# Weighted sums five blocks behind the scores, query tiles of 512 columns, six buffers of turned weights

## The chip, the cores and the metric

One core of a Trainium2 chip runs the program once. The metric is the device time of one execution in microseconds (us), given as the median of several runs. One execution was profiled; every time inside the program is read from that one.

The engines are PE (TensorE, matrix products and transposes), DVE (VectorE), ACT (ScalarE), POOL (GpSimd) and SP (SyncE, which here only issues DMA transfers). SBUF is the on-chip memory in which tiles lie, PSUM the accumulators of PE.

## What is computed

Attention with pooled keys, then a small network on the 128 highest-scoring rows of each batch:

```python
kv_pool = kv.reshape(B, H // r, r, W // r, r, C).mean(axis=(2, 4))   # B=4, H=384, W=32, r=4, C=128
k = v = kv_pool.reshape(B, -1, C) @ w_sr                              # 768 keys per batch
s = (q @ k.transpose(0, 2, 1)) / np.sqrt(C)                           # q: (4, 12288, 128)
a = np.exp(s - s.max(-1, keepdims=True))
a /= a.sum(-1, keepdims=True) + 1e-09
x = a @ v
...
for b in range(B):                                                    # capacity = 128
    top_idx = np.argpartition(-scores[b], capacity)[:capacity]        # scores = x . w_gate
    xe = x[b, top_idx]
    ye = np.maximum(xe @ w1, 0.0) @ w2                                # 128 -> 1024 -> 128
    out[b, top_idx] = xe + sigmoid(scores[b, top_idx])[:, None] * ye
```

## The kernel before

The 12288 queries of a batch are cut into 48 blocks of 256 columns (QT = 2 tiles of 128), 192 blocks over the four batches. One loop (lines 631 to 688) runs over the blocks. Iteration i does these things:

- On even i, `load_q` (line 135) issues the DMA that loads the queries of blocks i+8 and i+9 (512 columns, 256 KB) into a quarter of a query tile. A query tile holds 2048 columns, and pool `qp` has two of them.
- `s_max(i)`: DVE takes the negated row maxima of the scores (the TENSOR_REDUCE `m<-s`, one per block, so a block's start can be read from it).
- `AV(i - LAG, 0)` and `AV(i - LAG, 1)`: PE forms the weighted sums of the block LAG back, 36 matmuls of 128x130 into the one PSUM tile `o_two`. They need that block's weights turned by 90 degrees, tile `at`, and the values `vx`. LAG is 4 (line 630). While i < LAG, `warm` puts 36 matmuls of ones there instead (line 648).
- On even i, `split_q(i + 2)` splits the queries of two blocks into a high part (ACT, `qh`) and a low part (POOL, `ql`).
- `S(i + 1)`: PE forms the next block's scores, 12 matmuls of 512 or 256 columns (three passes of high and low parts), and between them, in batches 0 to 2, `turn_pe` turns two 128x128 pieces of the weights (`ae`) on PE.
- `exp(i, ...)` (ACT) forms the weights; `to_high` (ACT, `hl`) and `to_low` (POOL, and DVE for the part turned on PE) split them into a high and a low half of 16 bits. Line 402, `turn`, issues one DMA transpose per half, which turns `hl` into `at`. So each block has two DMA transposes, 384 in all.
- `sums`, `recip` and `finish` (DVE) divide `o_two` of block i - LAG by the row sums and put it into `x`; after every second block a DMA stores `x` (line 438) and POOL copies four columns of scores to `sc`.
- At fixed points (`at_point`) a step of a side task runs: the next batch's keys (`prep`: POOL sums `kv_sum`, then products), the first batch's values (`vals`), and `topk`, the choice of the 128 rows of a finished batch and the small network on them. `topk(b)` starts when the last block of batch b has been summed, that is in iteration 48(b+1) - 1 + LAG; its step in the next iteration forms sortable integers `key` from the scores with two DVE instructions on 128x96.

Every engine but SP executes in the order in which the code calls it. SP issues in order too, but the order of its issues is set by the scheduler when the program is built. Line 52 is the helper through which all compute instructions go, so nearly every row shows L52 and is told apart by its tile names.

The pools that hold a block's intermediate tiles are `hlp` (4 buffers of `hl`) and `at` (5 buffers). Before the loop `first_keys` loads the queries of the first 2048 columns as one transfer of 512 and one of 1536 columns. Behind the loop (lines 689 to 777) come the weighted sums of the last four blocks, into `o_all` (which is `o_two`) and into three spare pieces of the score buffers, then the choice of rows and the network for the last batch, partly by shorter steps of their own.

Of the kernel before, what the change touches and what calls it, by code (L numbers as in the profile page):

```python
# [6 lines left out]
F32 = mybir.dt.float32  # L7
# [12 lines left out]
P = 128  # L20
# [5 lines left out]
CHUNK = 2048  # L26
JPC = CHUNK // P
NCH = N // CHUNK
QT = 2
BLK = QT * P  # L30
NBLK = N // BLK
BPC = CHUNK // BLK
VC = C + 2
# [33 lines left out]
def attention_topk_mlp(ctx, tc, a, outs, capacity):  # L67
    nc = tc.nc
# [4 lines left out]
    kvp = ctx.enter_context(tc.tile_pool(name="kvp", bufs=3))  # L73
    kvs = ctx.enter_context(tc.tile_pool(name="kvs", bufs=2))
    keys = ctx.enter_context(tc.tile_pool(name="keys", bufs=2))
    qp = ctx.enter_context(tc.tile_pool(name="qp", bufs=2))
    qs = ctx.enter_context(tc.tile_pool(name="qs", bufs=3))
    wk = ctx.enter_context(tc.tile_pool(name="wk", bufs=3))
    wke = ctx.enter_context(tc.tile_pool(name="wke", bufs=2))
    hlp = ctx.enter_context(tc.tile_pool(name="hlp", bufs=4))  # L80
    at = ctx.enter_context(tc.tile_pool(name="at", bufs=5))
    ob = ctx.enter_context(tc.tile_pool(name="ob", bufs=3))
    sm = ctx.enter_context(tc.tile_pool(name="sm", bufs=4))
    tk = ctx.enter_context(tc.tile_pool(name="tk", bufs=2))
# [15 lines left out]
    s_buf = [ps_s.tile([P, KT, BLK], F32, name=f"s{i}") for i in range(2)]  # L100
# [3 lines left out]
    o_all = o_two[:, :, 0:VC]  # L104
# [15 lines left out]
    def load_kv(b, kc, parts=1, t=None):  # L120
        late = t is not None
        if not late:
            t = kvp.tile([P, 2, P // 2, TAPS], F32, name="kv_raw")
        n = 2 // abs(parts)
        for i in range(abs(parts)):
            if parts > 0 or late == (i > 0):
                nc.sync.dma_start(out=t[:, i * n:(i + 1) * n], in_=a["kv"][:, b, kc, i * n:(i + 1) * n])
        return t

    qraw = {}  # L130

    def load_q(b, ch, lo=0, hi=CHUNK):
        if (b, ch) not in qraw:
            qraw[b, ch] = qp.tile([P, CHUNK], F32, name="q_raw")
        nc.sync.dma_start(out=qraw[b, ch][:, lo:hi], in_=a["q"][:, b, ch, lo:hi])

    kvset = {}

    def new_keys(b):
        kvset[b] = {  # L140
            "kh": keys.tile([P, M], F32R, name="kh"),
            "kl": keys.tile([P, M], BF16, name="kl"),
            "kb": keys.tile([P, M], BF16, name="kb"),
            "raw": keys.tile([P, KT, 2, P], F32, name="kv_proj"),
            "vw": keys.tile([P, KT], F32, name="vw"),
            "mx": keys.tile([P, 4], F32, name="mx"),
            "vx": keys.tile([P, 2, KT, VC], F16, name="vx"),
            "sg": keys.tile([P, 4], F32, name="sg"),
        }

    def project(pooled, ps):
        pe.matmul(ps[:, 0], w_k, pooled, start=True, stop=True)
        pe.matmul(ps[:, 1], pooled, w_sr, start=True, stop=True)

    def split_k(b, lo, hi, part):
        kv = kvset[b]
        kh, kl, kb = (kv[k][:, lo * P:hi * P].rearrange("p (t k) -> p t k", k=P) for k in ("kh", "kl", "kb"))
        raw = kv["raw"][:, lo:hi, 0]
        if part == 0:
            act.copy(kh, raw)  # L160
            act.copy(kb, raw)
        else:
            kv["split"] = hi
            pool.tensor_tensor(out=kl, in0=raw, in1=kh.bitcast(F32), op=ALU.subtract)

    def v_gate(b, kc, v=None):
        u = kvs.tile([P, C], F32, name="vw_prod")
        dve.scalar_tensor_tensor(out=u, in0=kvset[b]["raw"][:, kc, 1] if v is None else v, scalar=1.0, in1=wg, op0=ALU.mult, op1=ALU.mult, accum_out=kvset[b]["vw"][:, kc:kc + 1])

    def v_max(b, pair):  # L170
        kv = kvset[b]
        dve.tensor_reduce(out=kv["mx"][:, pair:pair + 1], in_=kv["raw"][:, 2 * pair:2 * pair + 2, 1], axis=AX.XY, op=ALU.max, apply_absolute_value=True)
# [41 lines left out]

    def first_keys():
        new_keys(0)
        load_q(0, 0, 0, 2 * BLK)
        raws = [load_kv(0, kc) for kc in range(3)]
        nc.sync.dma_start(out=cst, in_=a["cst"])
        raws += [load_kv(0, kc, 2) for kc in range(3, KT)]  # L220
        load_q(0, 0, 2 * BLK, CHUNK)
        split_q(0, 0)
        kv = kvset[0]
        for kc in range(KT):
            pooled = kvs.tile([P, P], F32, name="pooled")
            for h in range(2):
                dve.tensor_reduce(out=pooled[:, h * P // 2:(h + 1) * P // 2], in_=raws[kc][:, h], axis=AX.X, op=ALU.add)
            if kc == 4:
                dve.tensor_copy(tri16, tri)
            if kc > 1:  # L230
                v_gate(0, kc - 2)
            if kc == 3:
                v_max(0, 0)
            ps = banks[kc % 2][:, 0:2 * P].rearrange("p (a b) -> p a b", a=2)
            if kc < KT - 1:
                project(pooled, ps)
                act.copy(kv["raw"][:, kc], ps)
                split_k(0, kc, kc + 1, 0)
                split_k(0, kc, kc + 1, 1)
            else:  # L240
                warm(4, banks[0][:, 0:P])
                project(pooled, ps)
                kh, kl, kb = (kv[k][:, kc * P:(kc + 1) * P] for k in ("kh", "kl", "kb"))
                dve.tensor_copy(kh, ps[:, 0])
                act.copy(kb, ps[:, 0])
                dve.tensor_tensor(out=kl, in0=ps[:, 0], in1=kh.bitcast(F32), op=ALU.subtract)
                act.copy(kv["raw"][:, kc, 1], ps[:, 1])
                warm(8, banks[1][:, 0:P])
        S(0)
        S(1)  # L250
# [67 lines left out]
    xt_ = {}  # L318

    def split_q(b, blk):  # L320
        ch, h = divmod(blk, BPC)
        raw = qraw[b, ch][:, h * BLK:(h + 2) * BLK]
        qh = qs.tile([P, 2 * BLK], F32R, name="qh")
        ql = qs.tile([P, 2 * BLK], BF16, name="ql")
        act.copy(qh, raw)
        pool.tensor_tensor(out=ql, in0=raw, in1=qh.bitcast(F32), op=ALU.subtract)
        for i in range(2):
            h, l = (x[:, i * BLK:(i + 1) * BLK] for x in (qh, ql))
            qsplit[b, blk + i] = h, h.bitcast(BF16).rearrange("p (q s) -> p q s", s=2)[:, :, 1], l

    blocks = [(b, blk) for b in range(B) for blk in range(NBLK)]
# [274 lines left out]
    blocks = [(b, blk) for b in range(B) for blk in range(NBLK)]  # L606
# [7 lines left out]
    def start(tasks, gen):  # L614
        tasks.append([gen, next(gen)])
# [11 lines left out]

    start(vals, first_values())
    nb = len(blocks)
    LAG = 4  # L630
    for i in range(nb):
        old = i >= LAG
        b, blk = blocks[i]
        if blk % 2 == 0 and i + BPC < nb:
            nb_, nblk = blocks[i + BPC]
            load_q(nb_, nblk // BPC, nblk % BPC * BLK, (nblk % BPC + 2) * BLK)
        if blk == 0 and b + 1 < B:
            start(prep, next_keys(b + 1))
        if i:
            borrow(s_flat[(i - 1) % 2])  # L640
        s_max(i)
        if old:
            AV(i - LAG, 0)
            at_point("pe")
            AV(i - LAG, 1)
        else:
            at_point("pe")
            warm(18 if i == 0 else 36, banks[0][:, 0:P])
        if i % 2 == 0 and i + 2 < nb:
            split_q(*blocks[i + 2])  # L650
        InOrder.seen.clear()
        at_point("ev")
        bank1 = list(InOrder.seen)
        InOrder.seen.clear()
        at_point("up")
        at_point("t")
        at_point("cmp")
        at_point("g")
        more = 0 < i < nb - 1
        bank0 = list(InOrder.seen)  # L660
        if more:
            S(i + 1, (3,), bank0 + bank1)
            S(i + 1, (2,), bank0)
        exp(i, 1)
        exp(i, 2)
        if by_pe(i):
            exp(i, 0)
            turn_pe(i)
        if more:
            S(i + 1, (1,), bank0)  # L670
            S(i + 1, (0,))
        to_high(i, 1)
        if old:
            sums(i - LAG)
            recip(i - LAG)
            finish(i - LAG)
        to_low(i, 1, dve)
        if not by_pe(i):
            exp(i, 0)
        to_high(i, 0)  # L680
        turn(i, 0)
        to_low(i, 0, pool)
        turn(i, 1)
        at_point("d")
        if i in (1, 2):
            advance(vals, "d")
        if old and blocks[i - LAG][1] == NBLK - 1:
            start(select, topk(blocks[i - LAG][0]))
    ended.append(True)
    room["select"], room["count"] = banks[1], banks[0][:, 0:1]  # L690
    n = nb - 1
    b = blocks[n][0]
    spare = [s_buf[(n + 1) % 2][:, 2 * k:2 * k + 2].rearrange("p k q -> p (k q)")[:, 0:QT * VC].rearrange("p (j c) -> p j c", j=QT) for k in range(3)]
    dest = {n - 3: o_all, n - 2: spare[0], n - 1: spare[1], n: spare[2]}

    def out(m):
        for j in range(QT):
# [20 lines left out]
    for j in range(3):  # L718
        pool.memset(jt[:, j:j + 1], float(j + 1))

    for m in (n - 3, n - 2):
        out(m)
        norm(m)
        put(m)
# [3 lines left out]
    for m in (n - 1, n):  # L728
        norm(m)
        lo = blocks[m][1] * QT  # L730
# [78 lines left out]
```

## Time and profile before

| | us |
|---|---|
| three runs | 977.23, 981.31, 986.22 |
| their median | 981.31 |
| the profiled execution, whole | 983.61 |
| its span, first to last record | 981.8 |
| PE busy | 908.2 (93 % of the span) |
| POOL busy | 749.9 (76 %) |
| ACT busy | 729.5 (74 %) |
| DVE busy | 699.7 (71 %) |

The busy share counts the time in which an engine has an instruction under way, waits left out. A row that ends in "[1.25 <-DMA at<-hl]" tells that the engine sat idle for 1.25 us before the instruction, and what ended that. "at<-hl" reads as "tile at, made from tile hl". The granted clock is TensorE's clock as a share of its full speed.

### The profile page before, as it was taken

Reading aid. Unit: us, or ns where it says so; the run is one execution under the profiler, and the core shown is the slowest. Engines: PE = TensorE matmul, PEld = TensorE weight load, DVE = VectorE, ACT = ScalarE, POOL = GpSimd, SP = SyncE. Lnnn points to the kernel's source line nnn. Section 1 sums busy time; section 2 is a strip of 40 time slices with the busy share of each in tenths; the row PEclk is TensorE's granted clock in tenths of the full one; section 3 lists DMA queues with packets and bytes.
Section 4 is the critical chain, followed back from the end, with each engine's and each line's share of the span. In section 5 each row is a group of like instructions: output and inputs, shape, how many; then the busy total and the mean of one; then the engine's idle time right before and its main releaser. Section 6 shows DMA issues by size and latency. Waiting matters only on the chain.

```text
span 981.8 us, 26115 instructions
## 1 busy us (share of the span) xinstructions
PE 908.2 (93%) x10067; PEld 729.7 (74%) x10067; DVE 699.7 (71%) x1732; ACT 729.5 (74%) x1177; POOL 749.9 (76%) x573
## 2 busy tenths in 40 slices
PE   3889999999989999998999998999999999999944
PEld 2668777787768787776787876877787887777743
DVE  6456666666668777776767776777768887878674
ACT  2567887877967877877877866878789988988700
POOL 1478889888778988987888887898778877777600
PEclk9999999999989999999999999999999999999966
DMA  9999999999999999999989999999999999999910
GB/s 357 227 190 220 241 220 224 244 242 236 225 203 186 249 226 219 233 230 225 235 169 210 236 218 226 207 199 203 199 184 245 224 242 244 231 235 234 225 40 6
DMA packets 600508, 211.31 MB, mean 215 GB/s; under 512 B 532288, under 2 KB 582592, under 8 KB 599616
## 3 DMA queue, kind: packets, MB, share of 16 engines
q1 hardware_dynamic: 600128, 209.12, 104.4%
q8 instruction: 79, 1.29, 0.6%
q0 software_dynamic: 256, 0.52, 0.2%
q14 instruction: 45, 0.37, 0.1%
HBM read 52.04 MB, written 25.43 MB: 79 GB/s over the span
## 4 chain that ended last, share of the span: by engine, by line
PE 56%; DVE 13%; ACT 9%; DMA 8%; issue 4%; POOL 3%; SPq 1%; POOLq 0%; ACTq 0%; DVEq 0%
PE s L52 31%; PE o_two L52 25%; DVE m L52 8%; DMA at<-hl 7%; ACT am L52 5%; POOL hl L52 1%; DVE junk L52 1%; ACT ae L52 1%; ACT hl L52 1%; ACT at L52 1%; POOL ql L52 1%; DVE at L52 1%; DMA xe<-out,idx 1%; POOL kv_sum L52 1%; ACT s L52 1%
## 5 line engine op out<-in xcount | busy, mean ns | idle before, releaser
L52 POOL TENSOR_TENSOR hl<-am,hl 128x1280 bf16<-128x1280 f32 x192 | 503.7, 2623 | 153.6 <-ACT hl L52 75.4
L52 PEld LDWEIGHTS <-at 128*128 128x128 f16 (+1 forms) x6912 | 415.5, 97 | 71.4 <-DMA at<-hl 22.5
L52 PE MATMUL o_two<-vx,at 128*128 128x130 f16 x6804 | 435.0, 220 | 17.5 <-DMA at<-hl 12.9
L52 ACT ACTIVATE am<-s,m 128x512 f32<-128x512 f32 (+1 forms) x384 | 305.4, 795 | 140.6 <-DVE m L52 80.9
L52 DVE TENSOR_REDUCE m<-s 128x2 f32<-128x1536 f32 x192 | 337.1, 1756 | 24.8 <-PE s L52 20.8
L52 PE MATMUL s<-kl,qh 128*128 128x512 bf16 (+1 forms) x768 | 253.3, 333 | 0.0
L52 PE MATMUL s<-kh,qh 128*128 128x512 f32 (+1 forms) x768 | 251.8, 409 | 0.0
L52 PE MATMUL s<-kb,ql 128*128 128x512 bf16 (+1 forms) x768 | 248.7, 327 | 0.5 <-POOL ql L52 0.4
L52 ACT CAST hl<-am 128x1280 f16<-128x1280 f32 x192 | 245.1, 1276 | 1.5
L52 DVE TENSOR_TENSOR at<-s,at 128x256 bf16<-128x256 f32 x144 | 61.1, 425 | 132.5 <-ACT at L52 124.4
L52 PEld LDWEIGHTS s<-kh,qh 128*128 128x128 f32 x768 | 131.6, 192 | 30.5 <-issue 0.6
L52 POOL TENSOR_TENSOR ql<-q_raw,qh 128x512 bf16<-128x512 f32 x96 | 122.5, 1276 | 6.8 <-ACT qh L52 6.8
L52 PEld LDWEIGHTS <-qh 128*128 128x128 bf16 x768 | 75.3, 98 | 63.2 <-issue 62.4
L52 DVE TENSOR_TENSOR x<-o_two,rz 128x260 f32<-128x260 f32 x189 | 81.0, 429 | 10.0
L52 PEld LDWEIGHTS <-ql 128*128 128x128 bf16 x768 | 76.2, 99 | 3.7 <-POOL ql L52 1.1
L52 DVE TENSOR_SCALAR rz<-o_two,sg 128x2 f32<-128x2 f32 x189 | 41.1, 218 | 40.2 <-PE o_two L52 39.3
L52 PE MATMUL s<-cst,ae 128*128 128x128 f32 x288 | 61.6, 296 | 8.4 <-ACT ae L52 7.7
L52 ACT ACTIVATE ae<-s,m 128x256 f32<-128x256 f32 x144 | 67.3, 467 | 0.0
L52 ACT CAST at<-s 128x256 f16<-128x256 f32 x144 | 54.5, 379 | 16.4 <-PE s L52 15.0
L52 ACT CAST qh<-q_raw 128x512 fp32r<-128x512 f32 x96 | 60.6, 631 | 1.1 <-DMA q_raw<-in_q 1.1
L52 PEld LDWEIGHTS s<-cst,ae 128*128 128x128 f32 x288 | 30.4, 141 | 32.0 <-ACT ae L52 31.4
L52 POOL TENSOR_TENSOR kv_sum<-kv_raw 128x256 f32<-128x256 f32 x72 | 52.4, 727 | 0.0
(164 smaller groups left out, 557.4 us busy)
## 6 DMA issues: line engine op xcount, KB each, us to landing
out<-x SPq DMA_DIRECT2D x96, 256.0 KB, 3.4
q_raw<-in_q SPq DMA_DIRECT2D x93, 256.0 KB, 3.8
kv_raw<-in_kv SPq DMA_DIRECT2D x36, 512.0 KB, 5.4
kv_raw<-in_kv SPq DMA_DIRECT2D x6, 1024.0 KB, 7.4
at<-hl SPq DMA_TRANSPOSE x384, 4.0
w<-in_w SPq DMA_DIRECT2D x2, 512.0 KB
q_raw<-in_q SPq DMA_DIRECT2D x1, 768.0 KB, 7.6
cst<-in_cst SPq DMA_DIRECT2D x1, 320.0 KB
```

Of the source, the lines that this page charges most:

```text
L52: r = f(*args, **kwargs)
```

## The change

LAG goes from 4 to 5, so that the weighted sums of a block run one iteration later, and `at` gets a sixth buffer for it. The queries come into tiles of 512 columns, one for each pair of blocks, in four buffers. The amount of data and the iteration in which a load is called are as before; a load takes a buffer of its own instead of a quarter of one, and the 1536 columns of the beginning become three transfers of 512. Behind the loop a fifth block is left to sum, into a fourth spare piece of a score buffer.

```diff
-    qp = ctx.enter_context(tc.tile_pool(name="qp", bufs=2))
+    qp = ctx.enter_context(tc.tile_pool(name="qp", bufs=4))
...
-    at = ctx.enter_context(tc.tile_pool(name="at", bufs=5))
+    at = ctx.enter_context(tc.tile_pool(name="at", bufs=6))
...
-    def load_q(b, ch, lo=0, hi=CHUNK):
-        if (b, ch) not in qraw:
-            qraw[b, ch] = qp.tile([P, CHUNK], F32, name="q_raw")
-        nc.sync.dma_start(out=qraw[b, ch][:, lo:hi], in_=a["q"][:, b, ch, lo:hi])
+    def load_q(b, blk):
+        ch, h = divmod(blk, BPC)
+        qraw[b, blk] = qp.tile([P, 2 * BLK], F32, name="q_raw")
+        nc.sync.dma_start(out=qraw[b, blk], in_=a["q"][:, b, ch, h * BLK:(h + 2) * BLK])
...
-        load_q(0, 0, 0, 2 * BLK)
+        load_q(0, 0)
...
-        load_q(0, 0, 2 * BLK, CHUNK)
+        for blk in range(2, BPC, 2):
+            load_q(0, blk)
...
-        raw = qraw[b, ch][:, h * BLK:(h + 2) * BLK]
+        raw = qraw.pop((b, blk))
...
-    LAG = 4
+    LAG = 5
...
-            nb_, nblk = blocks[i + BPC]
-            load_q(nb_, nblk // BPC, nblk % BPC * BLK, (nblk % BPC + 2) * BLK)
+            load_q(*blocks[i + BPC])
...
+    spare.append(s_buf[n % 2][:, 4:6].rearrange("p k q -> p (k q)")[:, 0:QT * VC].rearrange("p (j c) -> p j c", j=QT))
-    dest = {n - 3: o_all, n - 2: spare[0], n - 1: spare[1], n: spare[2]}
+    dest = {n - 4: o_all, n - 3: spare[0], n - 2: spare[1], n - 1: spare[2], n: spare[3]}
...
-    for m in (n - 3, n - 2):
+    for m in range(n - LAG + 1, n - 1):
```

What this does to the order of the instructions shows at three places.

On PE in iteration 4, in front of the scores of block 5 (`s_111`; `o_two` is the tile of weighted sums, `ones` a tile of ones):

```order
 L52 LDWEIGHTS ql
 L52 MATMUL s_110<-kb,ql 128x512
-L52 LDWEIGHTS at
-L52 MATMUL o_two<-vx,at 128x130
...
+L52 LDWEIGHTS ones_108
+L52 MATMUL o_two<-ones_108 128x128
...
 L52 LDWEIGHTS qh
 L52 MATMUL s_111<-kl,qh 128x512
```

The 36 pairs of the first weighted sums have left iteration 4 for iteration 5, and 36 pairs on ones stand there.

On SP, four blocks of the first batch; before:

```order
L402 DMA_TRANSPOSE at_1725<-hl_1724 128x10x128 x2
L135 DMA q_raw_2056<-in_q 128x512 x4
L402 DMA_TRANSPOSE at_1802<-hl_1801 128x10x128 x2
L438 DMA out_0<-x_1819 128x4x128
L402 DMA_TRANSPOSE at_1877<-hl_1876 128x10x128 x2
L402 DMA_TRANSPOSE at_1959<-hl_1958 128x10x128 x2
L438 DMA out_0<-x_1976 128x4x128
```

and after:

```order
L402 DMA_TRANSPOSE at_1732<-hl_1731 128x10x128 x2
L135 DMA q_raw_1910<-in_q 128x512
L438 DMA out_0<-x_1749 128x4x128
L402 DMA_TRANSPOSE at_1809<-hl_1808 128x10x128 x2
L402 DMA_TRANSPOSE at_1885<-hl_1884 128x10x128 x2
L135 DMA q_raw_2064<-in_q 128x512
L438 DMA out_0<-x_1902 128x4x128
L402 DMA_TRANSPOSE at_1967<-hl_1966 128x10x128 x2
```

The four loads of a query tile, which stood together between the transposes of two blocks, now stand one by one, one for every two blocks.

On POOL, about the start of the first batch's `topk` (`th` and `tl` are set at its start; on DVE its `key` pair stands behind the low half of block 52 before, of block 53 now; `hl_4252` and `hl_4267` are block 52's); before:

```order
L52 TENSOR_TENSOR hl_4170<-am_4169,hl_4170 128x1280
L52 TENSOR_TENSOR kv_sum_3895<-kv_raw_3890 128x256
L52 MEMSET th_4198 128x1
L52 MEMSET tl_4200 128x1
L52 TENSOR_TENSOR ql_4242<-q_raw_3264,qh_4241 128x512
L52 TENSOR_TENSOR hl_4252<-am_4251,hl_4252 128x1280
L52 TENSOR_TENSOR kv_sum_3895<-kv_sum_3895 128x128x4
```

and after:

```order
L52 TENSOR_TENSOR ql_4257<-q_raw_3741,qh_4256 128x512
L52 COPY sc_759<-x_4207 128x4
L52 TENSOR_TENSOR hl_4267<-am_4266,hl_4267 128x1280
L52 TENSOR_TENSOR kv_sum_3912<-kv_sum_3912 128x128x4
L52 MEMSET th_4294 128x1
L52 MEMSET tl_4296 128x1
L52 TENSOR_TENSOR hl_4343<-am_4342,hl_4343 128x1280
```

The start of `topk` has moved from the iteration that holds a `ql` to the next, which holds none.

## Rows read from the trace of the kernel before

**Rows 1.** The page: the span, each engine's busy time with its share and instructions.

```profile
span 981.8 us, 26115 instructions
PE 908.2 (93%) x10067; PEld 729.7 (74%) x10067; DVE 699.7 (71%) x1732; ACT 729.5 (74%) x1177; POOL 749.9 (76%) x573
```

**Rows 2.** The chain that ended last, one undisturbed block of batch 0 and the scores of a block of batch 3: start, duration, engine, tile, instructions.

```profile
183.32 2.06 PE o_two L52 x36
185.38 2.39 PE s L52 x14
...
754.84 2.03 PE s L52 x12
```

**Rows 3.** The waits of PE from 50 to 922 us: who waits <- for whom: us in all, times, longest.

```profile
PE o_two L52 <- DMA at<-hl: 12.9, 22, 2.2
...
PE s L52 <- ACT ae L52: 6.7, 11, 3.5
...
PE o_two L52 <- POOL vx L52: 2.5, 2, 2.2
```

**Rows 4.** The same view for three stretches: 400 to 470, 520 to 610 and 780 to 890 us, one row each.

```profile
PE o_two L52 <- DMA at<-hl: 3.0, 6, 1.4
...
PE o_two L52 <- DMA at<-hl: 4.7, 4, 2.2
...
PE o_two L52 <- DMA at<-hl: 4.5, 10, 1.2
```

**Rows 5.** The timeline of iterations 3 and 4: start, duration, engine, line, operation, tiles; in brackets the idle time before the row and what ended it.

```profile
45.66 2.17 PE L52 MATMUL o_two<-ones 128*128 128x128 bf16 x36
...
50.52 0.45 PE L52 MATMUL o_two<-vx,at 128*128 128x130 f16 x5
...
50.72 1.76 DVE L52 TENSOR_REDUCE m<-s 128x2 f32<-128x1536 f32 x1
...
54.02 0.65 POOL L52 TENSOR_TENSOR vx<-kv_proj,vx 128x256 f16<-128x256 f32 x1
...
54.72 2.52 PE L52 MATMUL o_two<-vx,at 128*128 128x130 f16 x27 [2.23 <-POOL vx L52]
...
60.35 1.76 DVE L52 TENSOR_REDUCE m<-s 128x2 f32<-128x1536 f32 x1 [0.20 <-PE s L52]
```

**Rows 6.** The view of tile `at`: its DMA transposes on SP, their duration there in ns (shortest, median, longest), first and last start.

```profile
L402 SPq DMA_TRANSPOSE at<-hl x384: 1252/1423/5044, 34.3 to 931.0; - x192
```

**Rows 7.** The timeline of SP's queue and of PE in the stretch up to 606 us, where the longest waits of batch 2 lie.

```profile
593.17 2.22 SPq L135 DMA_DIRECT2D q_raw<-in_q  x4
...
595.50 4.60 SPq L402 DMA_TRANSPOSE at<-hl  x2
...
604.41 0.52 PE L52 MATMUL o_two<-vx,at 128*128 128x130 f16 x6 [1.02 <-DMA at<-hl]
```

**Rows 8.** The waits of SP's query loads from 50 to 922 us, columns as in rows 3.

```profile
SPq L135 <- POOL ql L52: 4.8, 6, 1.2
```

**Rows 9.** Three windows, each with its length, then the busy time (instructions) of PE, PEld, DVE, ACT and POOL, the granted clock, the DMA share and GB/s.

```profile
55.40:58.80 3.40, 3.40 (x25) 2.66 (x22) 0.82 (x3) 0.00 (x0) 1.18 (x1) 0.50 0.73 182
...
284.00:291.00 7.00, 5.58 (x39) 4.59 (x40) 4.05 (x12) 4.93 (x9) 3.44 (x4) 0.51 1.18 214
...
604.90:608.40 3.50, 3.50 (x26) 2.77 (x23) 1.51 (x7) 0.12 (x1) 1.66 (x2) 0.51 1.18 263
```

**Rows 10.** The timeline about iteration 52, the start of the first batch's `topk`: DVE, POOL and one row of PE.

```profile
269.99 1.76 DVE L52 TENSOR_REDUCE m<-s 128x2 f32<-128x1536 f32 x1
...
274.45 1.76 DVE L52 TENSOR_REDUCE m<-s 128x2 f32<-128x1536 f32 x1
...
275.24 2.63 POOL L52 TENSOR_TENSOR hl<-am,hl 128x1280 bf16<-128x1280 f32 x1 [0.44 <-POOL sc L52]
...
278.58 1.28 POOL L52 TENSOR_TENSOR ql<-q_raw,qh 128x512 bf16<-128x512 f32 x1
...
278.78 1.15 DVE L52 TENSOR_SCALAR key<-sc 128x96 int32<-128x96 int32 x1
...
279.82 2.62 POOL L52 TENSOR_TENSOR hl<-am,hl 128x1280 bf16<-128x1280 f32 x1
...
279.96 2.59 DVE L52 TENSOR_TENSOR key<-key,sc 128x96 int32<-128x96 int32 x1
...
282.39 1.29 POOL L52 TENSOR_TENSOR kv_sum<-kv_sum 128x512 f32<-128x512 f32 x1
...
282.48 1.75 DVE L52 TENSOR_REDUCE m<-s 128x2 f32<-128x1536 f32 x1
...
285.42 0.69 PE L52 MATMUL s<-cst,ae 128*128 128x128 f32 x2 [3.48 <-ACT ae L52]
...
293.84 1.76 DVE L52 TENSOR_REDUCE m<-s 128x2 f32<-128x1536 f32 x1 [0.19 <-PE s L52]
```

**Rows 11.** The timeline of DVE in batch 1, the start of its `topk`: the second `key` instruction.

```profile
511.22 0.26 DVE L52 TENSOR_TENSOR key<-key,sc 128x96 int32<-128x96 int32 x1
```

**Rows 12.** The timeline of PE behind the loop: the weighted sums of the last blocks.

```profile
925.10 2.22 PE L52 MATMUL o_two<-vx,at 128*128 128x130 f16 x36 [0.97 <-DVE x L52]
...
933.36 0.85 PE L52 MATMUL s<-vx,at 128*128 128x130 f16 x12 [0.77 <-DMA at<-hl]
934.71 1.55 PE L52 MATMUL s<-vx,at 128*128 128x130 f16 x24 [0.49 <-DMA at<-hl]
```

More of the change, by code (lines that the diff above doesn't have):

```diff
@@ L320, in split_q @@
     def split_q(b, blk):
-        ch, h = divmod(blk, BPC)
-        raw = qraw[b, ch][:, h * BLK:(h + 2) * BLK]
+        raw = qraw.pop((b, blk))
         qh = qs.tile([P, 2 * BLK], F32R, name="qh")
```

## The prediction, made before the kernel was run

> **What bounds the kernel now.** The page first [rows 1]: PE is busy for 908.2 of 981.8 us, the others for about 700 to 750. So PE is the engine to follow, and 73.6 us in which it is idle are all that better order can win, besides stretches in which its clock is low. The profiled execution took 983.6 us, 2.3 above the median shown; the sum below is made against 983.6.
>
> Then the chain of waits, for one undisturbed block [rows 2]: 2.06 us of weighted sums and 2.39 us of scores follow each other, 4.45 us, and nothing else stands in the chain. In batch 3, without PE's transposes, the scores take 2.03, so a block takes some 4.1. The change removes no matrix product, so this floor stays. What can move lies in the blocks that take longer.
>
> The waits of PE inside the loop [rows 3] name three causes: turned weights that come late (12.9 us, 22 times), the transposes of `ae` that wait for ACT (6.7 us, of which one wait is 3.5), and the values' low half `vx` (2.5 us, two waits). I looked up where each lies. The late weights come in clusters: three stretches hold 3.0, 4.7 and 4.5 of the 12.9 us [rows 4]. The wait for `vx` is at the first weighted sums [rows 5]. The 3.5 us wait is at the start of the first batch's `topk` [rows 10].
>
> **Part 1: the first weighted sums move from iteration 4 to 5.** In iteration 4 PE began them at 50.52 and stopped; the last 27 matmuls waited 2.23 us for a `vx` that POOL had begun at 54.02 and took 0.65 us over, so it was there at 54.67 [rows 5]. The next row maximum came at 60.35, 9.63 us after the one of 50.72 [rows 5]; of that, 5.18 us are over the 4.45 of an ordinary block. Right after the wait the granted clock was 0.50, the 1.2 GHz level, for 3.4 us [rows 9], and this is inside the 9.63. Afterwards 36 matmuls of ones stand there, 2.17 us in the row of iteration 3 [rows 5], and wait for nothing. The first weighted sums begin about 50.5 + 4.45 = 54.95, later than 54.67. Gain: 5.2 us. Should they be called somewhat early, the wait is some tenths; if the clock falls all the same, 3.4 us at half speed give away 1.7. Bounds 3.3 to 5.2; I take 5.2, since the `vx` chain does not depend on the weighted sums.
>
> **Part 2: a block more of time for turned weights, and queries in single loads.** On SP four query loads take 2.22 us, and the two transposes behind them 4.60 [rows 7], where two median ones take 2.85 [rows 6]. So a group of four loads makes the transposes behind it about 2.22 + 1.75 = 4.0 us late, and the next group comes eight blocks on. Undisturbed, a block's two transposes and its share of two small loads and stores take some 3.4 us of SP (2.85, and half of 0.55 twice), so SP makes up about 1.0 us a block, and less beside the large key loads. That is how the waits come to stand in clusters: the queue does not run empty in between. Now one load stands between the transposes at a time; the same lateness comes in pieces of about 1 us, every second block. And a block's weights are needed 4.45 us later (4.1 in batch 3). A wait moves PE back, so within one cluster the waits add up to what the queue had fallen behind: 3.0, 4.7 and 4.5 us [rows 4]. Against 4.45, 4.45 and 4.1 this leaves 0.3 and 0.4 us, even without the evener loads. I take 11.9 of the 12.9 us as gained. Bounds: 3, if the queue falls behind as long as it is loaded (rival C), and 12.9.
>
> A query load must now wait until POOL has split the pair whose buffer it takes, and the transposes of the following blocks are queued behind it on SP. Such waits exist: 4.8 us in six [rows 8], the longest 1.2. With loads every second block they are more, but a transpose that is 1.2 us late has 4.45 us more to be so. I take nothing for it; without that cover it costs up to 1.2 each time. What would be late next is `hl`: it keeps four buffers, so a block's is wanted again four iterations on, now before its turned weights are.
>
> In batch 2 the clock fell after such a wait: 0.51 for 3.5 us from 604.9 [rows 9], behind the wait of 1.02 us at 604.41 [rows 7]. Without the wait it should stay up: 3.5 x 0.49 = 1.7 us gained (bounds 0 and 1.7).
>
> **Part 3: the start of the first `topk` moves by one iteration.** The row maxima of 274.45 and 293.84 lie 19.39 us apart, three blocks of 4.45 would be 13.35: 6.04 us were lost [rows 10]. The reason stands in the same rows. The two `key` instructions of DVE take 1.15 and 2.59 us; in batch 1 the second takes 0.26 [rows 11]. Here they lie under POOL's `ql` (278.58, 1.28 us) and `hl` (279.82, 2.62 us) and end with them. The row maximum slips to 282.48, ACT's `ae` comes late, PE waits 3.48 us, and the clock is 0.51 from 284 to 291 [rows 9, 10]. The Trainium skill, "SBUF — State Buffer", section "Who interferes with whom", says that VectorE and GpSimd share one port pair as an exclusive lock; by that rule, whichever starts first holds the other up, and the rows agree, 2.59 us instead of 0.26.
>
> Now `key` is formed in iteration 53, odd, without `ql`. What does POOL do there? In the odd iteration 51 `hl` began 275.24 - 269.99 = 5.25 us after the row maximum [rows 10], and `key` begins about 278.78 - 274.45 = 4.33 after it. Iteration 52's `hl` then ends at 5.25 + 2.62 - 4.45 = 3.4 us, and the `kv_sum` behind it, 1.29 us, at about 4.7. Between 4.7 and 5.25 lie 0.5 us, and the pair needs 0.20 + 0.26: it just fits. So this is a close race: gain 5.5 if it is won (some tenths of slip remain), about nothing if `hl` starts ahead of the second instruction. I take 5.5, and the other end is rival B. The starts of batches 1 and 2 move in the same way.
>
> **Part 4: behind the loop.** A block more is summed there, 2.06 us, and one more sum into a new piece waits for DVE's `x`, as the 0.97 us wait shows [rows 12], though the pieces are mostly free. Against this, the sums of the last two blocks now wait 0.77 + 0.49 us for their transposes [rows 12] and have more work ahead of them. And the loop loses one weighted sum (2.06) at its beginning, which the ones fill (2.17), so no time there. Net I take +1.5, bounds 0 and 3. The steps of batch 2's and 3's `topk` that run with it move by one step, some tenths either way.
>
> **Sum.** 983.6 - 5.2 - 11.9 - 1.7 - 5.5 + 1.5 = 960.8 us. The runs shown scatter from 977 to 986, as stalls that hang on a close race would; a version without the stalls ends where they are gone, so I don't move it by the 2.3 us to the median.
>
> **The rivals.**
> - *A, the forecast:* 952 to 964.5, chance 0.55. The lower end is where other small excesses go too (the waits of 0.2 to 1 us for `ae`, 3.2 us in all beyond the long one, and the tail at nothing).
> - *B, the race of part 3 is lost, there or at another start or end of `topk`:* one collision is 6.0 us, so 960.8 + 5.7 = 966.5. For it: both POOL spans press on a gap of 0.5 us. Against it: batch 1's start passed with 0.26 [rows 11]. Chance 0.25.
> - *C, SP or the DMA rings set the rate, and a block more only puts the waits off:* three quarters of the late weights stay, so part 2 gives 3 and no clock: 983.6 - 5.2 - 3 - 5.5 + 1.5 = 971.4. For it: a transpose took up to 5.0 us where 1.4 is the median [rows 6], and the bytes are the same. Against it: 3.4 us of 4.45 undisturbed, and the waits lie in three stretches, not everywhere [rows 4]. The Trainium skill, "DMA: Bandwidth & Descriptors", section "Latency and other measured facts", gives an effective 261 GB/s for a DMA transpose; an estimate by it for a block's 655,360 bytes is 2.5 us, which would speak against C as well. Chance 0.13.
> - *D, slower:* the new parity puts `topk`'s other DVE pairs under POOL's `hl`. There are six such places, the starts and the ends of the search in three batches, and each would cost 6.0 us with its clock. With k of them the time is about 960.8 + 6 k: four give 984.8, no faster than before, and six 996.8. For it: they all move together by one iteration, and a pair that lies under `hl` is ten times as long [rows 10, 11]. Against it: POOL's load differs from batch to batch, as the same pair in batch 1 shows. Chance 0.07.
>
> **How the numbers follow.** The likeliest is A, 960.8, and I put the time at 960.5. The range 952 to 973 holds A, B and most of C, some 0.85 with their edges taken off; what is left out is D and the ends. One per cent, 9.8 us, is about what a measurement of this kernel can tell from no change: faster lies below 971.5. A and B lie below it, and half of C; with their tails faster has 0.82. The rest of C and D up to four places make 0.13 for within 1%; more places than that, 0.05 for slower.
>
> **What would show it.** Right: PE goes through iterations 3 to 6 without a wait, and the row maxima of blocks 4 and 5 lie under 5 us apart (part 1). PE's waits for `at` are under 2 us in all, and SP's query loads stand singly (part 2). The second `key` instruction of batch 0 takes 0.26 us, and the clock is at 1.0 from 60 to 920 us (part 3). The end of the loop to the end of the span is 1 to 2 us longer than now (part 4). Wrong: waits for `at` of more than 5 us (C), `key` or the pair at the end of the search at 1 us or more (B, D), or ACT or POOL waiting for a free `hl`, which the sum holds at nothing.

## The result

| | median us | range | runs |
|---|---|---|---|
| before | 982.25 | 977.23 to 986.22 | 15 |
| changed | 988.39 | 982.13 to 990.74 | 15 |

The ratio is 1.006, with a 95 % interval of 1.0043 to 1.0078: 6 us slower where some 21 us faster was forecast, and 15 us above the top of the range. The profiled execution of the changed kernel took 988.03 us.

The page of the changed kernel, as [rows 1]:

```profile
span 986.3 us, 26072 instructions
PE 899.8 (91%) x9922; PEld 727.5 (74%) x10103; DVE 701.0 (71%) x1732; ACT 728.9 (74%) x1177; POOL 749.6 (76%) x573
```

PE's 899.8 us are too few: the page holds 9922 matmuls beside 10103 weight loads, where there were 10067 of each before, so 181 matmul records are missing.

The view of waits from 50 to 922 us (who waits <- for whom: us, times, longest), as [rows 3]:

```profile
ACT hl L52 <- DMA at<-hl: 39.8, 23, 3.8
...
PE o_two L52 <- DMA at<-hl: 12.5, 17, 1.7
PE s L52 <- ACT ae L52: 10.0, 20, 0.9
PE s L52 <- ACT am L52: 4.5, 7, 0.8
```

PE waits for turned weights as long as before, 12.5 us against 12.9, with a block more to spare. And there is a wait that was not there: ACT waits 39.8 us until a DMA transpose has read an `hl` and its buffer is free. PE's waits for ACT's `ae` and `am` hang on that in part; with a fifth buffer of `hl` (run 3) they are 5.3 and 0.2 us. The `vx` wait is gone.

The beginning, iterations 4 and 5, timeline of PE and DVE, as [rows 5]:

```profile
50.73 2.17 PE L52 MATMUL o_two<-ones 128*128 128x128 bf16 x36
...
50.93 1.76 DVE L52 TENSOR_REDUCE m<-s 128x2 f32<-128x1536 f32 x1
...
55.24 1.48 PE L52 MATMUL o_two<-vx,at 128*128 128x130 f16 x23
...
55.44 1.76 DVE L52 TENSOR_REDUCE m<-s 128x2 f32<-128x1536 f32 x1
```

The ones stand where the first weighted sums waited. The block takes 55.44 - 50.93 = 4.51 us instead of 9.63.

The start of the first `topk`, now in iteration 53, timeline of DVE and POOL, as [rows 10]:

```profile
275.21 1.76 DVE L52 TENSOR_REDUCE m<-s 128x2 f32<-128x1536 f32 x1
...
279.66 1.76 DVE L52 TENSOR_REDUCE m<-s 128x2 f32<-128x1536 f32 x1
...
283.20 1.29 POOL L52 TENSOR_TENSOR kv_sum<-kv_sum 128x512 f32<-128x512 f32 x1
...
283.99 0.63 DVE L52 TENSOR_SCALAR key<-sc 128x96 int32<-128x96 int32 x1
...
284.65 0.26 DVE L52 TENSOR_TENSOR key<-key,sc 128x96 int32<-128x96 int32 x1
...
284.83 1.75 DVE L52 TENSOR_REDUCE m<-s 128x2 f32<-128x1536 f32 x1
...
284.86 2.63 POOL L52 TENSOR_TENSOR hl<-am,hl 128x1280 bf16<-128x1280 f32 x1 [0.30 <-ACT hl L52]
```

The first `key` instruction lies under `kv_sum` until its end and takes 0.63 us, the second begins 0.21 us ahead of `hl` and takes 0.26 us. The race was won by about these 0.2 us: the block takes 284.83 - 279.66 = 5.17 us, 0.7 too many instead of 6.0.

So both gains came, some 10 us. They were lost again in many places: against blocks of 4.45 us (4.1 in batch 3), the batches 0, 1 and 3 lost 5.6, 9.0 and 4.4 us more than before from their ninth block on, and batch 2 lost 5.2 us less. One of these places, an ordinary block of batch 0, timeline of DVE, PE and ACT:

```profile
201.50 1.76 DVE L52 TENSOR_REDUCE m<-s 128x2 f32<-128x1536 f32 x1 [0.19 <-PE s L52]
...
202.61 0.85 PE L52 MATMUL o_two<-vx,at 128*128 128x130 f16 x12 [1.14 <-DMA at<-hl]
...
204.16 1.55 PE L52 MATMUL o_two<-vx,at 128*128 128x130 f16 x24 [0.70 <-DMA at<-hl]
...
204.22 1.26 ACT L52 CAST hl<-am 128x1280 f16<-128x1280 f32 x1 [3.36 <-DMA at<-hl]
...
208.03 1.76 DVE L52 TENSOR_REDUCE m<-s 128x2 f32<-128x1536 f32 x1
```

208.03 - 201.50 = 6.53 us, 2.1 over a block of 4.45. Both PE and ACT wait for transposes. So SP's queue is late by more than the new slack, and its timeline a little earlier shows what stands there, as [rows 7] (SPq is SP's queue; a row with x4 holds four issues one behind the other):

```profile
184.04 0.53 SPq L135 DMA_DIRECT2D q_raw<-in_q  x1
184.67 0.39 SPq L438 DMA_DIRECT2D out<-x  x1
185.17 7.20 SPq L402 DMA_TRANSPOSE at<-hl  x4
192.46 0.54 SPq L135 DMA_DIRECT2D q_raw<-in_q  x1
193.09 0.41 SPq L438 DMA_DIRECT2D out<-x  x1
193.55 0.49 SPq L127 DMA_DIRECT2D kv_raw<-in_kv  x1
```

A load and a store side by side, then four transposes, and no gap in the queue. The first of the four took 2.81 us by its own record, double the median of before. The view of tile `at`, as [rows 6] (duration on SP in ns: shortest, median, longest), has the median up from 1423 to 1532:

```profile
L402 SPq DMA_TRANSPOSE at<-hl x384: 1252/1532/5772, 36.1 to 937.4; - x192
```

SP shows where the slack went. I took every stretch of 40 transposes or more in which no gap between SP's issues is over 0.4 us, and divided its length by half its transposes; that is **SP's own pace**, the time that it takes for what belongs to a block. Before it was 4.43 us (three stretches, 130 of the 384 transposes), about PE's 4.45. Changed, it is 4.74 us (seven stretches, 288 transposes): there SP is the slower of the two, and falls behind by some 0.3 us with every block. Between such stretches it catches up: its gaps of over 0.4 us, from 30 to 940 us, add up to 64 us before and to 16 us changed.

### The profile page after: what moved, and what is told of

It is laid out like the page before. It is cut to its first block, busy times and chain, and to the rows that moved or that the text cites. A ratio compares the mean times of both kernels' runs of the same rounds, so it can differ in the third digit from the quotient of the medians.

```text
span 986.3 us, 26072 instructions
## 1 busy us (share of the span) xinstructions
PE 899.8 (91%) x9922; PEld 727.5 (74%) x10103; DVE 701.0 (71%) x1732; ACT 728.9 (74%) x1177; POOL 749.6 (76%) x573
## 4 chain that ended last, share of the span: by engine, by line
PE 46%; DVE 17%; DMA 13%; ACT 13%; issue 4%; POOL 4%; SPq 1%; POOLq 0%; ACTq 0%; DVEq 0%; another core or an unknown queue 0%
PE s L52 26%; PE o_two L52 20%; DMA at<-hl 11%; DVE m L52 10%; ACT am L52 7%; POOL hl L52 3%; ACT hl L52 2%; ACT ae L52 2%; DMA kv_raw<-in_kv 1%; DVE junk L52 1%; ACT at L52 1%; DVE at L52 1%; SPq L402 1%; ACT s L52 1%; DVE pooled L52 1%
## 5 line engine op out<-in xcount | busy, mean ns | idle before, releaser
L52 PE MATMUL o_two<-vx,at 128*128 128x130 f16 x6768 | 431.2, 219 | 15.1 <-DMA at<-hl 12.5
L52 PE MATMUL s<-kb,ql 128*128 128x256 bf16 (+1 forms) x697 | 221.5, 322 | 6.3 <-issue 0.2
L52 PE MATMUL s<-kl,qh 128*128 128x256 bf16 (+1 forms) x658 | 210.9, 324 | 0.0
```

Of the source, the lines that this page charges most:

```text
L52: r = f(*args, **kwargs)
```

## The experiments

Theory S was that lone query loads between the transposes make these longer; the rivals were that the lag only moves the wait (L), and that the DMA rings set one rate in any order (R). Each ratio is to the kernel before, measured in the same session, with its 95 % interval.

**1. The lag alone, with the old query tiles.** `hs` gets a pool of one buffer, which makes room in SBUF and is in all runs that need it.

```diff
-    LAG = 4
+    LAG = 5
...
-    at = ctx.enter_context(tc.tile_pool(name="at", bufs=5))
+    at = ctx.enter_context(tc.tile_pool(name="at", bufs=6))
```

> LAG 5 and six buffers of turned weights with the old query tiles of 2048 columns (the tile hs gets a pool of one buffer, to make room). Theory S (a lone query load between the transposes makes the transposes behind it longer; the new query tiles took what the lag gave): about 965 to 972 us, SP's queue with 30 us or more of idle time, ACT waiting under 10 us for a free hl. Theory L (the lag itself only moves the wait from the turned weights to the four buffers of hl): about 986 to 989 us, as the whole change, with ACT waiting some 30 to 40 us for hl. Theory R (the DMA rings set the rate in any order): 980 to 988 us.

974.59 us, ratio 0.9929 (0.9898 to 0.996). ACT waits 13.2 us for `hl`, PE 2.6 for turned weights. So the lag is no loss by itself; L is out, and R too. S came nearest, though it too had the time lower (to 972) and ACT's wait under 10 us.

**2. The query tiles alone, LAG 4.**

```diff
-    qp = ctx.enter_context(tc.tile_pool(name="qp", bufs=2))
+    qp = ctx.enter_context(tc.tile_pool(name="qp", bufs=4))
...
```

> The query tiles of 512 columns alone, LAG 4 and five buffers. Theory S: slower than before by 10 us or more, 992 to 1005 us, with PE's waits for turned weights at 25 us or more instead of 12.9, and a mean transpose of 1.85 us or more on SP instead of 1.77. Theory L: 980 to 984 us, as before. Theory R: 980 to 990 us.

972.68 us, ratio 0.9893 (0.9869 to 0.9918), and this is what no theory expected: S is out as well, and R a second time. PE's waits for turned weights are half of what they were, in the view from 50 to 905 us:

```profile
PE o_two L52 <- DMA at<-hl: 6.4, 9, 1.8
```

Each part makes the kernel faster, by 7 and 9 us, and both together slower by 6. Something arises only where they meet.

**3. The change with five buffers of `hl`.**

```diff
-    hlp = ctx.enter_context(tc.tile_pool(name="hlp", bufs=4))
+    hlp = ctx.enter_context(tc.tile_pool(name="hlp", bufs=5))
...
```

> The change with a fifth buffer of hl (and the tile hs in a pool of one buffer, to make room). Theory L: the 40 us of ACT's waits for hl go, and with them the time falls to 965 to 975 us. Theory S: ACT's waits go, but SP is as far behind as before, so the waits come back at the turned weights: 982 to 988 us. Theory R as S.

987.79 us, ratio 1.0054 (1.0032 to 1.0077), so L is out a second time. ACT's waits for `hl` went, the time didn't, and PE still waits for turned weights, from 50 to 922 us:

```profile
PE o_two L52 <- DMA at<-hl: 11.3, 14, 1.7
```

So the four buffers of `hl` are where the lateness shows, not where it comes from. The profiled execution was the fastest of the twelve, with 977.38 us, so its waits are rather short for this run.

**4. The change with loads of 1024 columns.**

```diff
...
-        if blk % 2 == 0 and i + BPC < nb:
-            load_q(*blocks[i + BPC])
+        if blk % 4 == 2 and i + 6 < nb:
+            load_q(*blocks[i + 6])
```

> The change with query tiles of 1024 columns in two buffers, so half as many query loads, each of 512 KB, and the same SBUF. Theory S: half of the lone loads, so the loss of the new tiles halves: about 975 to 980 us. Theory L and theory R: 985 to 989 us, as the change.

978.28 us, ratio 0.9948 (0.9929 to 0.9968), as S had it, though S can't explain run 2. With half as many loads, beside half as many stores, 10.1 of the 15.7 us between the change and run 2 are won back.

**The new theory.** The order of SP's issues differs between run 2 and the change. With LAG 4 the store follows an odd iteration's sums, and the load an even iteration's split, so they alternate: two transposes, load, two transposes, store. With LAG 5 the store falls to even iterations too and lands beside the load; with the old tiles the loads stand in other places (in run 1, 64 of the 96 stores stand alone between transposes, in the change 5). Two copies side by side, theory P, would be what costs. The runs 5 and 6 set the place alone, by an ordering rule on the load (`turned` holds the transposes of each block):

```diff
+        if behind in turned:
+            tc.add_manual_dep(
+                r.ins, turned[behind].ins.name,
...
-            load_q(*blocks[i + BPC])
+            load_q(*blocks[i + BPC], i - 2)
```

**5. The change, load and store apart.**

> The whole change, but each query load is held behind the transposes of one block more, so that on SP load and store alternate (two transposes, load, two transposes, store) as in the run of the tiles alone, and don't stand side by side. Theory P (place: with LAG 5 the store falls to the same place of SP's queue as the load, and two copies side by side make the transpose behind them longer): about 958 to 966 us, the transpose behind a load or a store back at a median of 1.35 to 1.5 us, SP idle for 40 us or more. Theory Q (the two parts want the same slack of the DMA rings, and place does not matter): 983 to 989 us, as the change. Theory H (the four buffers of hl are what bounds LAG 5): 980 us or more, with ACT waiting 20 us or more for hl.

966.41 us, ratio 0.9849 (0.982 to 0.9878). Waits from 50 to 922 us, where a wait of `o_two` for turned weights no longer appears (the 1.2 us at `s` are behind the loop, which ends at about 910 us):

```profile
ACT hl L52 <- DMA at<-hl: 7.6, 7, 1.5
...
PE s L52 <- DMA at<-hl: 1.2, 2, 0.6
```

and its SP, with one copy at a time:

```profile
105.37 3.67 SPq L407 DMA_TRANSPOSE at<-hl  x2
109.09 0.57 SPq L135 DMA_DIRECT2D q_raw<-in_q  x1
109.77 3.01 SPq L407 DMA_TRANSPOSE at<-hl  x2
112.87 0.53 SPq L443 DMA_DIRECT2D out<-x  x1
113.51 2.80 SPq L407 DMA_TRANSPOSE at<-hl  x2
```

SP's pace is 4.53 us. The number and the size of the transfers are those of the change. Q and H are out. P holds, with a time 0.4 us over its range; SP's gaps of over 0.4 us, from 30 to 940 us, are 43 us.

**6. The tiles alone, load and store put together.** The same rule with LAG 4, where it has the opposite effect.

> The tiles alone with LAG 4, but each query load is held behind the transposes of one block more, which puts it beside the store (load, store, four transposes), as in the whole change. Theory P: it loses what the tiles alone gave and more, 985 to 1000 us, and the first transpose behind the pair takes a median of 2.1 us or more. Theories Q and H: 970 to 975 us, as the tiles alone.

997.34 us, ratio 1.0175 (1.0136 to 1.0214): 24.7 us more than run 2, from which it differs only by the place of the loads. Its waits, 50 to 905 us, and its SP:

```profile
PE o_two L52 <- DMA at<-hl: 22.8, 24, 5.8
```

```profile
186.01 0.57 SPq L135 DMA_DIRECT2D q_raw<-in_q  x1
186.68 0.40 SPq L443 DMA_DIRECT2D out<-x  x1
187.17 7.39 SPq L407 DMA_TRANSPOSE at<-hl  x4
```

Read as a square, it gives the place and the lag apart from each other:

| us | load and store apart | together |
|---|---|---|
| LAG 4 (new tiles) | 972.68 | 997.34 |
| LAG 5 (new tiles) | 966.41 | 988.39 |

The place is worth 25 and 22 us, the lag 6 and 9. The four times are from three sessions, in which the kernel before had 981.4 to 982.3 us.

Two other causes would fit run 5 alone. A load that is held for a block no longer waits until POOL has freed its buffer; but SP's gaps ahead of its loads (over 0.25 us, from 50 to 905 us) are 3.2 us in the change and 0.5 in run 5, against 13.2 us in run 2, which is fast, and 0.5 in run 6, the slowest. And with load and store together four transposes follow each other; but the third and the fourth of them have medians of 1.36 to 1.41 us in the change and in run 6, and it is the first that is long.

**7. Run 5 with five buffers of `hl`.**

> As the run with load and store apart and LAG 5, with a fifth buffer of hl. Theory P: within 4 us of that run, since SP is seldom more than four blocks behind. Theory H: faster than it by 8 us or more.

966.58 us, ratio 0.9849 (0.9821 to 0.9876), the same as run 5. H is out a second time.

**8. LAG 6, nothing held.** Its edit is that of run 1 one step further, on the changed kernel: seven buffers of `at` and a sixth place behind the loop.

> The change with LAG 6 and seven buffers of turned weights (hs in a pool of one buffer), nothing held in its place: with an even lag the store falls to the other blocks again, and load and store alternate by themselves. Theory P (place): 960 to 969 us, near the run with load and store held apart. If it is not the place but something in the holding of the loads that made that run fast, or if the lag itself is bad: 985 us or more.

979.08 us, ratio 0.9977 (0.996 to 0.9994): neither. On SP load and store alternate by themselves, its pace is 4.52 us, and no weighted sum waits for turned weights. So far theory P held. But PE waits elsewhere, from 50 to 922 us:

```profile
PE s L52 <- ACT ae L52: 10.4, 9, 4.5
...
PE s L52 <- DVE oh L52: 5.3, 3, 2.3
```

and the start of batch 1's `topk`, which stands in an even iteration again, shows why (DVE and POOL):

```profile
508.44 1.76 DVE L52 TENSOR_REDUCE m<-s 128x2 f32<-128x1536 f32 x1
...
512.54 1.01 POOL L52 DMA_INDIRECT out<-xo,idx  x1 [0.15 <-POOL kv_sum L52]
...
513.09 4.51 DVE L52 TENSOR_TENSOR key<-key,sc 128x96 int32<-128x96 int32 x1
...
513.65 1.27 POOL L52 TENSOR_TENSOR ql<-q_raw,qh 128x512 bf16<-128x512 f32 x1
...
514.87 2.61 POOL L52 TENSOR_TENSOR hl<-am,hl 128x1280 bf16<-128x1280 f32 x1
...
517.53 1.75 DVE L52 TENSOR_REDUCE m<-s 128x2 f32<-128x1536 f32 x1
```

4.51 us for an instruction of 0.26: it began under POOL's indirect store, 0.56 us ahead of `ql`, and ended with `hl`, so the block takes 9.09 us. That is the mechanism of the prediction's part 3, at another batch. It is so at four blocks, which take 2.8 to 4.6 us longer than in run 5, 13.7 in all (the two profiled executions lie 8.9 us apart, 977.27 and 968.38), and behind each the granted clock is 0.50 for 3.4 us: the starts of `topk` in batches 0 and 1, and twice a pair `oh` where the rows are picked, 2.95 us under POOL's `hl` where run 5 has 0.60 (DVE and POOL of run 8):

```profile
460.98 2.95 DVE L52 SCALAR_TENSOR_TENSOR oh<-cst,ecx,ge 96x128 bf16<-96x128 f32 x2
...
461.13 2.65 POOL L52 TENSOR_TENSOR hl<-am,hl 128x1280 bf16<-128x1280 f32 x1 [0.23 <-ACT hl L52]
```

**9. LAG 5, two loads side by side every fourth block, no store beside them.** Against run 5:

```diff
-        if blk % 2 == 0 and i + BPC < nb:
-            load_q(*blocks[i + BPC], i - 2)
+        if blk % 4 == 2:
+            for k in (i + BPC - 2, i + BPC):
+                if k < nb:
+                    load_q(*blocks[k], i - 2)
```

> LAG 5, the loads away from the stores, but two loads side by side behind every fourth block's transposes, so half as many pairs of copies as in the change, and none of a load and a store. Theory P1 (any two copies side by side cost): 970 to 980 us, with the first or second transpose behind a pair of loads at 1.9 us or more. Theory P2 (only a load beside a store costs): 963 to 969 us, as with load and store apart.

968.43 us, ratio 0.9864 (0.9848 to 0.988), 2 us over run 5. The first transpose behind a pair of loads has a median of 2.04 us (28 of them from 100 to 640 us without a gap), as P1 says; the time is P2's, and SP's pace of 4.55 us is about run 5's. Whether a store beside a load is worse than a load beside a load stays open: here the pairs are half as many, and the slack of LAG 5 may cover them.

**10. Run 5 with each load in two halves of 128 KB, one behind each transpose of a block.**

> LAG 5, load and store apart, and each load in two halves of 128 KB, one behind each transpose of the block. If what counts is how much copying stands in one place: 960 to 965 us, and the transposes behind a half load under 1.45 us on the mean. If a lone load is already small enough: 964 to 968 us, or some us more, since 96 more transfers are issued.

983.58 us, ratio 1.0014 (0.999 to 1.0038), 17 us over run 5, against both expectations. The first halves take SP 0.53 us and the second 0.57 (medians), as long as a whole load, and SP's pace is 4.65 us. So two half loads take SP some 0.5 us more than one whole load, for every two blocks: it pays by the transfer (a load of 512 KB in run 4 took it 0.53 us too). Nor did halving shorten the transposes: the first one behind a lone half load has a median of 1.50 us. But both halves of about a third of the loads (35) still stand side by side here, so the loss is not split between more transfers and two of them in one place.

The runs in one table. "Behind a copy" is the median of the first transpose behind a load and then a store, or behind a lone load / a lone store (of those from 100 to 640 us that follow without a gap; 42 pairs in the change, 43 in run 6).

| run | us | load and store | behind a copy, us | SP's pace, us |
|---|---|---|---|---|
| before | 982.25 | mostly apart, loads in fours | store 1.34 | 4.43 |
| the change | 988.39 | together | 2.25 | 4.74 |
| 1, lag alone | 974.59 | mostly apart, loads often in groups | 1.45 / 1.35 | 4.61 |
| 2, tiles alone | 972.68 | apart | 1.36 / 1.34 | 4.53 |
| 3, five `hl` | 987.79 | together | 2.27 | 4.67 |
| 4, loads of 1024 | 978.28 | together, half as many loads | 2.14 | 4.57 |
| 5, held apart | 966.41 | apart | 1.38 / 1.34 | 4.53 |
| 6, held together | 997.34 | together | 2.32 | 4.66 |
| 7, 5 with five `hl` | 966.58 | apart | 1.41 / 1.35 | 4.53 |
| 8, LAG 6 | 979.08 | apart | 1.38 / 1.34 | 4.52 |
| 9, loads in pairs | 968.43 | apart | two loads 2.04 / store 1.35 | 4.55 |
| 10, half loads | 983.58 | apart, some halves in pairs | 1.50 / 1.35 | 4.65 |

The long transpose goes with the place in every run. The pace does not rank the kernels by itself: it is lowest before, where lateness comes in lumps instead, as the second transpose behind four loads has a median of 3.13 us (ten groups from 100 to 640 us). And behind a lone load a part of the price falls on the second transpose, 1.59 us in run 5, so that the means of the four transposes of two blocks add up to 6.8 us in the change and to 6.3 in run 5.

## Why the prediction was wrong

**Part 1, right.** It said 5.2 us at the first weighted sums; the block went from 9.63 to 4.51 us, 5.1. The granted clock is 1.00 there instead of 0.50.

**Part 2, wrong, and this is the step that failed.** The prediction put "the same lateness comes in pieces of about 1 us, every second block" and reckoned "3.4 us of SP" for an undisturbed block, so that SP makes up 1.0 us a block. Two things are wrong in it. First, undisturbed durations were summed: two median transposes make 2.85 us, but the mean over all 384 before is 1.76, so 3.5 a block, and where the queue ran without a gap its pace was 4.43 us already before, no reserve beside PE's 4.45. The row of the longest transposes [rows 6] hinted at that, and it was the argument for rival C. Second, the loads were taken as lone ones. The order of SP's issues, in the section on the change, shows them beside a store, though the text there calls them "one by one", and the prediction costed that place at nothing. Runs 5 and 6 show its price: 22 us with LAG 5, 25 us with LAG 4. This second error is the one that decided: in run 5 the pace is 4.53 us, no better than before, and still a block of lag covers it. The forecast gain of 11.9 us became 0.4 at the turned weights (12.9 to 12.5), and ACT's new waits for `hl` came on top. The prediction named `hl` as "what would be late next" and held it at nothing; run 3 shows that more buffers don't help while SP is the slower. The load's wait for POOL, also held at nothing, was no cause (3.2 us in the change). And the 11.9 is a slip: 0.3 and 0.4 off 12.9 leave 12.2.

The mechanism beside it was right: with the load held apart (run 5) the waits of the weighted sums for turned weights are gone, and the 966.4 us are 6 above the forecast. What the 6 us are was not tested; about as much is in PE's waits for ACT, of which the sum held 3.2 us (for `ae`, beyond the long one); in run 5 they are 11.1, from 50 to 905 us:

```profile
PE s L52 <- ACT ae L52: 7.0, 18, 0.8
PE s L52 <- ACT am L52: 4.1, 8, 0.8
```

**The clock, half right.** The low stretch at 604 us is gone with the wait ahead of it, but another came at 440.7 us, right behind a wait of 1.70 us for turned weights, at 0.50, the 1.2 GHz level; so nothing is gained by it. As [rows 9]:

```profile
440.70:444.00 3.30, 3.08 (x27) 3.03 (x28) 1.14 (x7) 3.30 (x5) 1.97 (x1) 0.50 1.25 299
```

In run 5 the granted clock is 1.00 from 39.4 to 905 us.

**Part 3, right.** 5.5 us were forecast; 6.0 of excess became 0.7, so 5.3. The race was as narrow as it said. By the Trainium skill, "SBUF — State Buffer", section "Who interferes with whom", an instruction of VectorE may be held by GpSimd's; run 8 agrees, with 4.51 us instead of 0.26. That whichever starts first holds the other up does not show there: `key` began 0.56 us ahead of `ql`, and `ql` took its usual 1.27 us; whether the indirect store before them already held it is open. Rival B is what LAG 6 met.

**Part 4, right in sign, within its bounds.** +1.5 was forecast. From the last row maximum of the loop to the end of the span it is 60.3 us before (981.8 - 921.5) and 60.5 changed (986.3 - 925.8), so +0.2. The weighted sums behind the loop, as [rows 12], wait once more for `x` than before, and one wait for a transpose is left:

```profile
928.92 2.22 PE L52 MATMUL o_two<-vx,at 128*128 128x130 f16 x36 [1.10 <-DVE x L52]
...
934.23 2.22 PE L52 MATMUL s<-vx,at 128*128 128x130 f16 x36 [1.03 <-DVE x L52]
937.43 2.90 PE L52 MATMUL s<-vx,at 128*128 128x130 f16 x48 [0.98 <-DVE x L52]
940.88 1.55 PE L52 MATMUL s<-vx,at 128*128 128x130 f16 x24 [0.55 <-DMA at<-hl]
```

**The rivals.** C came nearest, as SP's pace bounds long stretches. But its mechanism, that a block more only puts the waits off, is not what happened: with the lag alone (run 1) the waits for turned weights fell from 12.9 to 2.6 us. C also assumed the pace to stay as it was; the change itself made it worse, and so the time ended above all but rival D's. D itself, `topk` at a new parity, did not happen with LAG 5. The estimate of 2.5 us a block, by the Trainium skill, "DMA: Bandwidth & Descriptors", section "Latency and other measured facts", spoke against C; no run here shows the transposes' rate by itself. SP's pace, copies included, was 4.4 to 4.7 us.

**What stays open.** Why a transpose behind two copies takes SP longer was not found; the runs show the place and the price. The two sides of run 9 are not told apart, and both forecasts for run 10 were too low.

## What to carry to other kernels

When a queue issues without gaps, its pace is read from the stretches without gaps, not from the sum of undisturbed durations; if that pace is near the busiest engine's, whatever lengthens it eats the slack ahead of it: here a block of slack covered 4.53 us a block, and did not cover 4.74. Before changing how far one stage runs behind another, look at what else falls into the same iteration, in the issue order of every queue: here, with the new tiles, the parity of the lag alone put a store beside a load, and a second time `topk` beside POOL's split. Two changes that are each worth 7 to 9 us can lose 6 together, so each is worth measuring alone.

## What the runs showed of the hardware

Two 256 KB copies issued side by side took SP 0.53 and 0.40 us (medians in the change), but the DMA transpose right behind them a median of 2.25 us, 2.32 in run 6, where one behind a lone copy takes 1.34 to 1.38 (runs 2, 5 and 8). A load of half the size took SP as long as a whole one (0.53 and 0.57 us against 0.57, runs 10 and 5). And a DVE instruction of 0.26 us took 4.51 us across the end of a POOL indirect store and two POOL instructions (run 8), so one collision can be longer than a single POOL instruction.
